# Forward substitution in VectorE's lanes on 16x16 blocks, two to a lane, instead of 32x32, with the block under the diagonal made by small TensorE products

## The chip, the cores and the metric

One core of one Trainium2 chip runs the whole program. The metric is the device time of one execution in microseconds. The kernel before takes 839.43 us in the median of three runs (832.2 to 842.1).

## The reference

An attention layer with a recurrent state is followed by an MLP. For each of 4 x 8 (batch, head) pairs the state is a 40 x 40 matrix; 768 steps of time update it:

```python
y[:, :, t] = np.einsum('bhd,bhde->bhe', rt, state)
Sa = np.einsum('bhde,bhe->bhd', state, at)
state_decay = state * wt[:, :, None, :] - np.einsum('bhd,bhe->bhde', Sa, bt)
state = state_decay + np.einsum('bhd,bhe->bhde', vt, kt)
```

The MLP takes the 3072 rows of 320 values: `h = x @ w_in`, `g = h * tanh(softplus(h))`, `out = g @ w_out`, with a width of 2048 between. All data is f32.

## The kernel before

**Chunks.** Time is cut into 12 chunks of 64 steps. Within a chunk the recurrence is written as matrix products, which needs the inverse of a triangular 64x64 matrix for each pair of batch and head. That matrix is handled as two diagonal 32x32 blocks, which are inverted, and a block under them, which is made by products.

**Three kinds of work.** `pre_a(c, be)` (line 126) prepares chunk c for half of the pairs: it loads w, a, b and k, forms the running products of the decay by scans on VectorE (lines 147 and 157), scales a (152) and b, k (170), stores the decays (172, through the POOL queue), and makes on TensorE (186) the products of a with b and k, from which the triangular matrices go to `gp` (lines 188, 189, 193), other parts to `ha` (190, 191). `inv(n)` (line 381) inverts the matrices of chunks 2n and 2n+1 at once; it is `pre_inv(n)` followed by `post_inv(n)`. `step(c)` (line 349) carries the state through chunk c: L284 multiplies the matrices KT with the state, L314, L334 and L339 make the chunk's output and the new state, L346 writes the state ST; step c+1 needs it.

**The inversion.** In `pre_inv` (line 205) a transpose by 32x32 blocks on VectorE (L209) brings the 128 matrices of 32x32 into lanes, one matrix to each of the 128 partitions: the tile X (named XL) is [128, 32, 32]. L210 writes ones on the diagonal. The loop of lines 211 to 216 is forward substitution: for i from 1 to 30 it multiplies column i under the diagonal with row i (L214, into `tmp`) and adds the (31-i) x i products (L216), each instruction waiting for the one before. L218 transposes back to TT, L220 also writes the plain transpose of half of it to T1, in place over a part of `gp`.

`post_inv` (line 223) makes, for each of the two chunks (h), 32 products of 32x32 (L232), a copy of them by ScalarE (L235), 32 more (L241), puts the blocks together in `bdT` (L249, L250 from TT, L251 from the products), multiplies with `ha` (L258) and copies the result to KT (L260), which `step` reads at L284.

**Buffers.** X, TT and `tmp` have one buffer each (`NXL`, `NTT`, `NTMP` are 1), `gp` two. The PSUM pool `ps_a` has two banks (`NA = 2`), which all products of `post_inv` share.

**Order.** The program is written down as step 2n, `pre_a` for the chunks of pair n + 2, `inv(n + 1)`, step 2n + 1 (`ORDER`, line 36). A scheduler then orders each engine's instructions by priority and by its estimate of what is ready; each engine carries them out in that fixed order. `at(tc, k)` gives the instructions under it the offset `OFF[k]` (line 38) in that priority: 80 for every inversion (`'I'`), and one of its own for each (`I0` 600, `I1` -15, and so on). Once the last `pre_a` is done, its memory is freed and the MLP's weights are loaded and split into two parts (lines 453 to 495); the MLP then follows, 12 pieces of 256 rows.

Of the kernel before, what the change touches and what calls it, by code (L numbers as in the profile page):

```python
# [7 lines left out]
F32 = mybir.dt.float32  # L8
F32R = mybir.dt.float32r
AF = mybir.ActivationFunctionType  # L10
ALU = mybir.AluOpType
# [20 lines left out]
NTMP = 1  # L32
# [4 lines left out]

OFF = {'I': 80, 'T1': 80, 'P00': -40, 'P10': 80, 'P11': 40, 'b0': 15, 'c0': 600, 'u0': -15, 'u1': 250, 'd0': 250,
       'd1': 150, 'W': 600, 'V': 400, 'E': 150, 'I0': 600, 'I1': -15, 'I2': 15, 'I3': 150, 'I4': 80, 'p4': 15,
# [4 lines left out]
def at(tc, k):  # L44
    return tc.high_priority(offset=OFF[k]) if OFF.get(k) else nullcontext()
# [33 lines left out]
def attention(ctx, tc, I, yD, pD, nch, M):  # L79
    nc = tc.nc  # L80
    V, A, PE, SP, G = nc.vector, nc.scalar, nc.tensor, nc.sync, nc.gpsimd
# [4 lines left out]
    ps_a = pool("ps_a", NA, ictx, "right", space=PSUM)  # L86
# [4 lines left out]
    ci = pool("ci", 1, ictx)  # L91
    iw = pool("iw", 2, ictx)
# [9 lines left out]
    bkb = [cp.tile([128, 8, 168], F32, name=f"bk{i}") for i in range(NWA)]  # L102
    adb = [cp.tile([128, 8, 2, 2, 32], F32, name=f"ad{i}") for i in range(NAD)] * (2 // NAD)
    d1 = cp.tile([128, 584], F32, name="d1")
    bdT = [ci.tile([128, 8, 2, 64], F32, name=f"bdT{i}") for i in range(2)]
    z = cs.tile([128, 1], F32, name="z")
    V.memset(z, 0.0)
# [97 lines left out]
    def pre_inv(n):  # L205
        gp = GP[n]

        X = iw.tile([128, 32, 32], F32, name="XL", bufs=NXL)
        V.transpose(X.rearrange("p t j -> p j t"), gp[:, :, 1].rearrange("p u j -> p j u"))  # L209
        V.memset(X.rearrange("p t j -> p (t j)")[:, 0:1024:33], 1.0)  # L210
        for i in range(1, 31):
            tmp = iw.tile([128, 240], F32, name="tmp", bufs=NTMP)
            tv = tmp[:, 0:(31 - i) * i].rearrange("p (t j) -> p t j", j=i)
            V.tensor_tensor(out=tv, in0=X[:, i + 1:32, i:i + 1].broadcast_to([128, 31 - i, i]),  # L214
                            in1=X[:, i:i + 1, 0:i].broadcast_to([128, 31 - i, i]), op=ALU.mult)
            V.tensor_tensor(out=X[:, i + 1:32, 0:i], in0=X[:, i + 1:32, 0:i], in1=tv, op=ALU.add)  # L216
        TT = iw.tile([128, 32, 32], F32, name="TT", bufs=NTT)
        V.transpose(TT.rearrange("p u t -> p t u"), X)  # L218
        T1 = gp[0:64, :, 0]
        V.transpose(T1, TT[0:64])  # L220
        return TT, T1

    def post_inv(n, TT, T1):
        gp = GP[n]
        for h in range(2):
            with at(tc, 'T%d' % h):
# [10 lines left out]
                for j in range(16):  # L237
                    u = h * 16 + j
                    for al in range(2):
                        q = slice(al * 32, 32 + al * 32)  # L240
                        PE.matmul(py[q, j], T1[q, u], X[q, j], start=(j == 0), stop=True, skip_group_check=True)  # L241
                for be in range(2):
# [138 lines left out]
    def inv(n):  # L381
        with at(tc, 'I%d' % n), at(tc, 'I'):
            TT, T1 = pre_inv(n)
        with at(tc, 'J%d' % n):
            post_inv(n, TT, T1)
# [93 lines left out]
class Mlp:  # L479
# [6 lines left out]
    def pool(self, n, b, side="right", **k):  # L486
        return self.ctx.enter_context(self.tc.tile_pool(name=n, bufs=b, side=side, **k))
# [140 lines left out]
def build(tc, I, out, nch):  # L628
    with ExitStack() as ctx:
        dp = ctx.enter_context(tc.tile_pool(name="dp", bufs=1, space=bass.MemoryType.DRAM))  # L630
        yD = dp.tile([nch, 2, 40, 2, 512], F32, name="yD")
        pD = dp.tile([nch, 2, 40, 2, 520], F32, name="pD")
        M = Mlp(ctx, tc, I, yD, pD, out)
        with ExitStack() as actx:
            attention(actx, tc, I, yD, pD, nch, M)
        M.run(nch)
# [21 lines left out]
```

## Time and profile before

| | |
|---|---|
| median of three runs | 839.43 us (832.2 to 842.1) |
| span of the profiled execution, first to last instruction | 843.5 us |
| mean granted TensorE clock over it | 0.939 |
| VectorE in L214 and L216, all six inversions | 58.5 and 59.0 us, 180 instructions each |
| TensorE in L232 and L241 | 768 records each |
| ScalarE busy | 429.0 us (51%) |

The profiled execution's time is its span; a separate clock of that one execution is not at hand, so it stands beside the runs, 4.1 us above their median.

In a profile, PE is TensorE's matmul, PEld its weight loads, DVE VectorE, ACT ScalarE, POOL GpSimd, SP SyncE. A group's line gives line, engine, operation, out<-in, partitions x elements, count, busy us, mean ns of one, and the idle time ahead of it with what ended it. A timeline's line gives start and duration in us, and in brackets the idle time before. A stretch's line gives its bounds and length, then for each engine the busy us and the number of instructions, then the granted TensorE clock, the share of the DMA engines and GB/s. In the rows of slices each digit is the busy share, in tenths, of a fortieth of the span (21 us).

### The profile page before, as it was taken

The page shows a single profiled execution, that of the slowest core. Times are in us where ns is not written, and L with a number is a line of the kernel's source. Part 1 is how long each engine was busy: PE and PEld are TensorE (multiplying, and loading weights), DVE is VectorE, ACT ScalarE, POOL GpSimd, SP SyncE. Part 2 cuts the span into 40 slices and gives each one's busy share as a digit, 9 for nine tenths or more (in the row PEclk, how much of TensorE's full clock was granted, in tenths as well). Part 3 has the DMA queues.
Part 4 walks back from the last instruction along what each step waited for, and adds up shares of the span by engine and source line. Part 5 has one row for each costly group of instructions (what it writes and reads, how often), then busy time and mean ns, then how long its engine had stood idle before and what let it go on. Part 6 is the DMA issues. An engine that isn't in the chain of part 4 may idle for free.

```text
span 843.5 us, 18796 instructions
## 1 busy us (share of the span) xinstructions
PE 748.6 (89%) x7816; PEld 695.6 (82%) x7816; DVE 462.0 (55%) x975; ACT 429.0 (51%) x937; POOL 103.3 (12%) x182
## 2 busy tenths in 40 slices
PE   2645898998989889889799899999999999999998
PEld 2534697887868778778768799999999999999998
DVE  6789879739899658788924639221222222122110
ACT  4533647774586866566738546333333333333331
POOL 8100012113122023221101200000000000000000
PEclk9855689899999999899959999999999999999999
DMA  6422223323423233323425734211120111100000
GB/s 177 134 71 64 74 63 73 90 67 105 129 81 80 66 88 103 82 67 96 123 66 142 179 109 128 54 35 36 38 54 25 31 54 35 35 21 16 16 1 32
DMA packets 58212, 61.91 MB, mean 73 GB/s; under 512 B 25536, under 2 KB 48704, under 8 KB 58128
## 3 DMA queue, kind: packets, MB, share of 16 engines
q1 hardware_dynamic: 49296, 40.94, 17.6%
q0 software_dynamic: 8832, 19.79, 9.5%
q8 instruction: 61, 1.00, 0.5%
q14 instruction: 23, 0.19, 0.1%
HBM read 48.79 MB, written 11.86 MB: 72 GB/s over the span
## 4 chain that ended last, share of the span: by engine, by line
PE 62%; DVE 15%; ACT 15%; issue 5%; DMA 2%; ACTq 0%; DVEq 0%; SPq 0%
PE ph L583 21%; PE po L604 7%; PE po L605 7%; PE po L603 7%; PE pa L186 5%; PE pa L258 4%; PE pq L314 3%; PE pq L334 2%; DVE XL L216 2%; DVE tmp L214 2%; ACT ad L155 2%; PE pu L284 1%; DMA cv_d<-in_wo 1%; DVE P L147 1%; ACT bdT L250 1%
## 5 line engine op out<-in xcount | busy, mean ns | idle before, releaser
L583 PE MATMUL ph<-xh,w_ih 128*128 128x256 f32 x576 | 148.3, 283 | 0.5 <-ACT xh L566 0.5
L585 ACT ACTIVATE g<-ph 128x512 f32<-128x512 f32 x96 | 57.3, 598 | 179.3 <-PE ph L583 179.2
L589 DVE TENSOR_TENSOR gl<-g,gh 128x1024 fp32r<-128x1024 f32 x48 | 58.7, 1225 | 160.7 <-ACT gh L588 160.4
L583 PE MATMUL ph<-xh,w_il 128*128 128x256 f32 x576 | 123.6, 283 | 0.0
L186 PE MATMUL pa<-bk,ad 128*128 128x168 f32 x384 | 85.0, 373 | 42.7 <-DVE bk L170 15.0
L604 PE MATMUL po<-w_ol,gh 128*128 128x320 f32 x384 | 118.8, 310 | 0.1
L605 PE MATMUL po<-w_oh,gl 128*128 128x320 f32 x384 | 118.4, 309 | 0.0
L603 PE MATMUL po<-w_oh,gh 128*128 128x320 f32 x384 | 117.7, 309 | 0.0
L186 PEld LDWEIGHTS pa<-bk,ad 128*128 128x128 f32 x384 | 70.8, 233 | 47.8 <-issue 22.8
L583 PEld LDWEIGHTS ph<-xh,w_ih 128*128 128x128 f32 x576 | 109.3, 190 | 0.7 <-ACT xh L566 0.7
L583 PE MATMUL ph<-xl,w_ih 128*128 128x256 f32 x384 | 101.2, 285 | 0.0
L583 PEld LDWEIGHTS ph<-xh,w_il 128*128 128x128 f32 x576 | 96.3, 190 | 0.0
L583 PEld LDWEIGHTS ph<-xl,w_ih 128*128 128x128 f32 x384 | 73.1, 190 | 0.8 <-issue 0.5
L604 PEld LDWEIGHTS po<-w_ol,gh 128*128 128x128 f32 x384 | 72.1, 188 | 0.5 <-DVE w_ol L495 0.5
L605 PEld LDWEIGHTS po<-w_oh,gl 128*128 128x128 f32 x384 | 72.1, 188 | 0.1
L603 PEld LDWEIGHTS po<-w_oh,gh 128*128 128x128 f32 x384 | 71.8, 188 | 0.0
L258 PE MATMUL pa<-bdT,HA 128*104 128x128 f32 x384 | 57.0, 304 | 9.0 <-ACT bdT L251 7.3
L258 PEld LDWEIGHTS pa<-bdT,HA 128*104 128x104 f32 x384 | 49.9, 190 | 14.4 <-ACT bdT L251 9.1
L216 DVE TENSOR_TENSOR XL<-XL,tmp 128x30 f32<-128x30 f32 (+9 forms) x180 | 59.0, 328 | 2.4
L214 DVE TENSOR_TENSOR tmp<-XL 128x30 f32<-128x30 f32 (+9 forms) x180 | 58.5, 325 | 2.5
L314 PE MATMUL pq<-bdr,UVT 128*128 128x128 f32 x384 | 57.3, 294 | 2.3 <-DVE UVQ L316 1.5
L314 PEld LDWEIGHTS pq<-bdr,UVT 128*128 128x128 f32 x384 | 50.8, 205 | 4.0 <-DVE UVQ L316 1.9
(89 smaller groups left out, 1243.5 us busy)
## 6 DMA issues: line engine op xcount, KB each, us to landing
wa<-in_wa SPq DMA_DIRECT2D x48, 162.5 KB
bk<-in_bk SPq DMA_DIRECT2D x48, 160.0 KB
cv_d<-in_wi SPq DMA_DIRECT2D x12, 512.0 KB
cv_d<-in_wo SPq DMA_DIRECT2D x8, 640.0 KB
pD<-P POOLq DMA_DIRECT2D x48, 81.2 KB, 2.2
VS<-in_vN POOLq DMA_DIRECT2D x24, 160.0 KB, 3.6
UVT<-in_vD POOLq DMA_DIRECT2D x24, 160.0 KB, 3.9
bdr<-in_rD POOLq DMA_DIRECT2D x24, 160.0 KB, 4.4
```

Source lines behind the costliest of these rows:

```text
L155: A.copy(ad[q, :, :, al], a[q].rearrange("p (s k t) -> p s k t", k=2, t=32))
L186: PE.matmul(pt[:, j], ad[:, s0 + j].rearrange("p k a t -> p (k a t)"), bk[:, s0 + j], start=(j == 0), stop=True, skip_group_check=True)
L214: V.tensor_tensor(out=tv, in0=X[:, i + 1:32, i:i + 1].broadcast_to([128, 31 - i, i]), in1=X[:, i:i + 1, 0:i].broadcast_to([128, 31 - i, i] ...
L216: V.tensor_tensor(out=X[:, i + 1:32, 0:i], in0=X[:, i + 1:32, 0:i], in1=tv, op=ALU.add)
L258: PE.matmul(pk[:, j], ha[:, s0 + j], bd[:, s0 + j].rearrange("p a t -> p (a t)"), start=(j == 0), stop=True, skip_group_check=True)
L314: PE.matmul(pq[:, s], UVT[:, g * 4 + s, be * 128:be * 128 + 128], br[:, be, g * 4 + s].rearrange("p a t -> p (a t)"), start=(s == 0), stop ...
L583: PE.matmul(o, w, x, start=(j == 0 and n == 0), stop=(n == 7), skip_group_check=True)
L585: A.activation(g[:, f0:f0 + 2], ph, AF.Mish)
L589: V.tensor_tensor(out=gl, in0=g, in1=gh.bitcast(F32), op=ALU.subtract)
L603: PE.matmul(po[k], gh[:, j, t], oh, start=(f == 0), stop=False, skip_group_check=True)
L604: PE.matmul(po[k], gh[:, j, t], ol, start=False, stop=False, skip_group_check=True)
L605: PE.matmul(po[k], gl[:, j, t], oh, start=False, stop=(f == 15), skip_group_check=True)
```

## The change

The forward substitution runs on the two 16x16 blocks of the diagonal of each matrix at once: the access pattern's first free dimension is [528, 2], which steps from one block to the other (16 rows of 32 and 16 columns further), and the loop goes from 1 to 14. The lower left block of X is cleared first. L218 then gives a TT that has the two small inverses. The inverses' left columns are also transposed into a new tile TD (whose other columns stay zero). Two batches of 128 TensorE products of 32x32 with 16 columns, one product for each matrix, with a ScalarE copy between them, make the block under the diagonal in PSUM: the first multiplies the matrix in `gp` with columns 16 to 31 of TT, the second TD with the result. VectorE adds the second batch to TT. Both batches take their PSUM banks from `ps_a`; the copy X1 goes to the first half of X. T1 and `post_inv` follow as before.

```diff
@@ attention
+    TD = ci.tile([128, 32, 32], F32, name="TD")
+    G.memset(TD, 0.0)
@@ pre_inv
         V.memset(X.rearrange("p t j -> p (t j)")[:, 0:1024:33], 1.0)
-        for i in range(1, 31):
-            tmp = iw.tile([128, 240], F32, name="tmp", bufs=NTMP)
-            tv = tmp[:, 0:(31 - i) * i].rearrange("p (t j) -> p t j", j=i)
-            V.tensor_tensor(out=tv, in0=X[:, i + 1:32, i:i + 1].broadcast_to([128, 31 - i, i]),
-                            in1=X[:, i:i + 1, 0:i].broadcast_to([128, 31 - i, i]), op=ALU.mult)
-            V.tensor_tensor(out=X[:, i + 1:32, 0:i], in0=X[:, i + 1:32, 0:i], in1=tv, op=ALU.add)
+        V.memset(X[:, 16:32, 0:16], 0.0)
+
+        for i in range(1, 15):
+            m = 15 - i
+            tmp = iw.tile([128, 112], F32, name="tmp", bufs=NTMP)
+            tv = tmp[:, 0:2 * m * i].rearrange("p (b t j) -> p b t j", b=2, j=i)
+            x = X[:, 0:1, 0:1]
+            ap = lambda t, j, st, sj: bass.AP(x.tensor, x.offset + 32 * t + j, [x.ap[0], [528, 2], [st, m], [sj, i]])
+            V.tensor_tensor(out=tv, in0=ap(i + 1, i, 32, 0), in1=ap(i, 0, 0, 1), op=ALU.mult)
+            V.tensor_tensor(out=ap(i + 1, 0, 32, 1), in0=ap(i + 1, 0, 32, 1), in1=tv, op=ALU.add)
         TT = iw.tile([128, 32, 32], F32, name="TT", bufs=NTT)
         V.transpose(TT.rearrange("p u t -> p t u"), X)
+        V.transpose(TD[:, :, 0:16].rearrange("p u j -> p j u"), X[:, :, 0:16].rearrange("p t j -> p j t"))
+        px = ps_a.tile([128, 32, 16], F32, name="pa")
+        for u in range(32):
+            for q in (slice(g * 32, g * 32 + 32) for g in range(4)):
+                PE.matmul(px[q, u], gp[q, u, 1], TT[q, u, 16:32], start=(u == 0), stop=True, skip_group_check=True)
+        X1 = X.rearrange("p t j -> p (t j)")[:, 0:512].rearrange("p (u t) -> p u t", t=16)
+        A.copy(X1, px)
+        py = ps_a.tile([128, 32, 16], F32, name="pa")
+        for u in range(32):
+            for q in (slice(g * 32, g * 32 + 32) for g in range(4)):
+                PE.matmul(py[q, u], TD[q, u], X1[q, u], start=(u == 0), stop=True, skip_group_check=True)
+        V.tensor_tensor(out=TT[:, :, 16:32], in0=TT[:, :, 16:32], in1=py, op=ALU.add)
         T1 = gp[0:64, :, 0]
         V.transpose(T1, TT[0:64])
         return TT, T1
```

## The prediction

> **What bounds the kernel now.** I read the page first (busy time, slices), then a table of stretches cut at the six inversions, then the groups of VectorE's instructions by shape, then the timeline around the places where a recurrence step starts. From the page:
>
> ```profile
> span 843.5 us, 18796 instructions
> ...
> PE 748.6 (89%) x7816; PEld 695.6 (82%) x7816; DVE 462.0 (55%) x975; ACT 429.0 (51%) x937; POOL 103.3 (12%) x182
> ...
> PE   2645898998989889889799899999999999999998
> ...
> DVE  6789879739899658788924639221222222122110
> ...
> POOL 8100012113122023221101200000000000000000
> ```
>
> The 55% of VectorE is a mean over two halves: from slice 24 on (the MLP) TensorE is full and VectorE has a fifth of its time in use; ahead of it (attention) VectorE is at 7 to 9 tenths, and TensorE too. So the change, which touches attention only, must be priced there. The stretches below begin with a transpose into `XL` and end with the transpose at L220 (the two bounds of an inversion), but for the last, the MLP:
>
> ```profile
> core 0: us, PE busy (x) PEld busy (x) DVE busy (x) ACT busy (x) POOL busy (x), PEclk, DMA share, GB/s
> 49.90:100.50 50.60, 27.32 (x164) 22.68 (x164) 47.00 (x118) 20.30 (x59) 5.07 (x10) 0.62 0.23 69
> 100.50:153.50 53.00, 48.48 (x640) 43.22 (x634) 45.44 (x113) 35.01 (x90) 9.95 (x18) 0.88 0.31 75
> 186.80:237.20 50.40, 43.55 (x565) 38.48 (x563) 47.64 (x127) 29.26 (x81) 15.23 (x27) 1.00 0.41 109
> 237.20:280.60 43.40, 37.33 (x594) 32.45 (x594) 40.03 (x104) 32.01 (x80) 8.56 (x16) 1.00 0.27 75
> 321.30:370.80 49.50, 44.83 (x503) 39.89 (x504) 43.86 (x117) 27.09 (x75) 12.91 (x23) 0.93 0.33 80
> 370.80:419.60 48.80, 41.37 (x727) 36.72 (x726) 41.80 (x107) 36.10 (x84) 7.82 (x12) 0.97 0.40 112
> 485.00:843.50 358.50, 354.75 (x2758) 353.51 (x2757) 95.59 (x102) 130.42 (x190) 1.00 (x2) 1.00 0.15 42
> ```
>
> VectorE is busy for 47.0 of 50.6 us in the first inversion, 47.6 of 50.4 in the third, 86 to 92% in the others. But TensorE is at 85 to 91% in all except the first (54%); its busy time is modelled, so I read this as "close to full", not full. Two engines bind in turn.
>
> Does the end of an inversion start anything? These rows are from the timeline: the state of the step before (ST), the KT that comes from the inversion, and the first matmul of the next step (L284).
>
> ```profile
> 235.60 0.48 DVE L346 TENSOR_TENSOR ST<-stn,R 128x320 f32<-128x320 f32 x1
> 246.00 0.55 PEld L284 LDWEIGHTS pu<-KT,VS 104*64 104x64 f32 x16 [0.18 <-ACT KT L260]
> ...
> 314.06 0.49 DVE L346 TENSOR_TENSOR ST<-stn,R 128x320 f32<-128x320 f32 x1
> 315.78 0.28 PE L284 MATMUL pu<-KT,VS 104*64 104x64 f32 x2
> ...
> 370.77 0.44 DVE L346 TENSOR_TENSOR ST<-stn,R 128x320 f32<-128x320 f32 x1
> 380.06 0.58 ACT L260 COPY KT<-pa 104x512 f32<-104x512 f32 x1 [0.74 <-PE pa L258]
> 381.66 1.12 PE L284 MATMUL pu<-KT,VS 104*64 104x64 f32 x16
> ```
>
> Step 4 starts 9.9 us after its state was there, released by KT: the inversion sets it. Step 8 likewise starts 10.5 us after its state, just behind KT. Step 6 starts 1.2 us after the state: there the recurrence sets the time and not the inversion.
>
> **VectorE, per inversion.** Groups by line and shape:
>
> ```profile
> L216 DVE TENSOR_TENSOR XL<-XL,tmp 128x30 f32<-128x30 f32 (+9 forms) x180 | 59.0, 328 | 2.4
> L214 DVE TENSOR_TENSOR tmp<-XL 128x30 f32<-128x30 f32 (+9 forms) x180 | 58.5, 325 | 2.5
> ...
> L214 DVE TENSOR_TENSOR tmp<-XL 128x30 f32<-128x30 f32 x12 | 2.1, 176 | 0.2
> L216 DVE TENSOR_TENSOR XL<-XL,tmp 128x108 f32<-128x108 f32 x12 | 3.2, 268 | 0.2
> ...
> L209 DVE STREAM_TRANSPOSE XL<-GP 128x1024 f32<-128x1024 f32 x6 | 12.7, 2124 | 0.0
> L218 DVE STREAM_TRANSPOSE TT<-XL 128x1024 f32<-128x1024 f32 x6 | 11.8, 1970 | 0.1
> L316 DVE TENSOR_TENSOR UVQ<-pq,cst 128x512 f32<-128x512 f32 x48 | 32.9, 688 | 24.4 <-PE pq L314 24.3
> L109 DVE MEMSET wa<- 128x1040 f32 x2 | 1.9, 925 | 0.4 <-issue 0.4
> ```
>
> Removed: 60 instructions, (59.0 + 58.5) / 6 = 19.6 us. Added in their place: 28 of 2(15-i)i elements, 28 to 112 (1120 in all for each of the two lines). From 176 ns at 30 and 268 at 108 elements an instruction costs 141 ns and 1.18 ns per element: 28 x 0.141 + 2240 x 0.00118 = 6.6 us. The clear of 16 x 16 is a quarter of L109's elements, 0.25 us. TD is the transpose of half a tile: half of 1.97 to 2.12, 1.0 us. The closing add reads 512 elements from PSUM as L316 does: 0.69 us. Net -19.6 + 6.6 + 0.25 + 1.0 + 0.69 = -11.1 us for each of 6 inversions, 66 us of VectorE. That price is sure to about 1 us. The one clear of TD goes to POOL at the start, where the slices show 8 tenths for 21 us and next to nothing after; TD is first read after 53 us, so I cost it at nothing (a few us if its place in the queue held up a load).
>
> **TensorE, per inversion.** 256 products of 32x32 weights with 16 columns. Lines 232 and 241 make 32 such products with 32 columns per half, and the trace has 64 records for them: an f32 product is two records. So 512 records are added. Rows of the timeline, the first inversion and the last, and the group of the ScalarE copy between two such batches:
>
> ```profile
> 99.24 1.82 PE L232 MATMUL pa<-TT,GP 32*32 32x32 f32 x64 [0.24 <-DVE TT L218]
> ...
> 418.23 1.20 PE L232 MATMUL pa<-TT,GP 32*32 32x32 f32 x64 [0.30 <-DVE TT L218]
> ...
> L235 ACT COPY X<-pa 64x512 f32<-64x512 f32 x12 | 6.9, 575 | 0.2
> ```
>
> 64 records take 1.20 us at full clock, 1.82 in the first inversion, where the table shows a clock of 0.62. At these prices 512 cost 9.6 us (14.6 in the first): 62 us in all. The new batches go round four tiles instead of two and stream half the columns, which no row here shows; the lower bound is half the price, 4.8 us, the upper one is under rival 2. I take 9.6, the nearest row.
>
> **Latency.** Nothing after an inversion may use TT before the add. Behind the transpose to TT now come 4.8 us (first batch), 0.58 (copy to X1, on ScalarE as L235), 4.8 (second batch), 0.69 (add): 10.9 us at full clock, 15.9 in the first inversion. TD's transpose lies beside the first batch. The loop in front is 13.0 us shorter (19.6 - 6.6). So a lone inversion would end 2 us earlier, 3 later in the first. What can be gained beyond that comes from other VectorE work that is laid into those 11 to 16 us: the first stretch has 47.0 us busy, of which the inversion's own transposes and loop make
>
> ```profile
> sum 285.30, DVE 141.92; mean DVE 23.65
> ```
>
> 23.65 us (the view of the stretches for tile XL alone), so 23 us of other work to lay there. The add is a new wait on VectorE: it stands there until the last product, and in order behind it wait whatever the scheduler put next, the masks of line 191 (which free TensorE's other banks) and those of L316 (which the steps need) first of all; the 0.69 us are charged, such a blockage is part of rival 3. The new batches take the two `ps_a` banks in turn, and X is free only after the second batch; the next inversion's L209 stands behind that, but it starts later than this anyway in every case before (187 against 153, 321 against 281), except for the second, fourth and sixth, which follow within 5 us.
>
> **The sum, stretch by stretch.** First: VectorE-bound, TensorE half idle: -11.1, of which 3 are lost as uncovered latency: -8; nothing runs ahead of step 0, so all of it comes through. Second: 11.1 off an engine with 7.6 us idle, 9.6 on one with 4.5 idle: 0. Third: step 4 can move by at most 9.9, and TensorE pays 9.6: -5, half of it. Fourth: step 6 waits for the state, so VectorE's relief is worth nothing; a third of TensorE's 9.6 falls between matmuls of steps 4 and 5: +3. Fifth: as the third, with more TensorE time: -4. Sixth: a third of 9.6 again: +3. Products that the scheduler lays one by one between other matmuls (rival 2): 15 in all at 0.34, +5. Sum -8 + 0 - 5 + 3 - 4 + 3 + 5 = -6 us. The MLP's 358.5 us stay. The profiled execution's span of 843.5 becomes 837.5; it stands 4.1 above the median of 839.4 (its runs go from 832.2 to 842.1), so on the median's scale I forecast 833.4 us.
>
> **Rival 1: the small products cost little.** If four tiles run at once, a batch takes half (4.8 us per inversion): the latency falls to 6 us, and the stretches become -9, -4, -8, 0, -6, 0, with no charge for interleaving: -27, 812 us. For it: the 16 columns, the four row groups. Against: the rows of 64 in 1.20 us already have two tiles. [...] Chance 0.22.
>
> **Rival 2, slower: products laid one by one between other matmuls.** Where the scheduler alternates them, the timeline shows
>
> ```profile
> 395.54 0.94 PE L334 MATMUL pq<-UVQ,bkn 128*64 128x104 f32 x16
> ...
> 422.14 0.39 PE L334 MATMUL pq<-UVQ,bkn 128*64 128x104 f32 x2
> 422.46 0.24 PE L241 MATMUL pa<-X,GP 32*32 32x32 f32 x2
> 422.64 0.39 PE L334 MATMUL pq<-UVQ,bkn 128*64 128x104 f32 x2
> 422.96 0.24 PE L241 MATMUL pa<-X,GP 32*32 32x32 f32 x2
> ```
>
> From 422.14 to 422.64 is one pair of each: 0.50 us, against 0.12 (0.94 / 8) and 0.04 (1.20 / 32) in a block: 0.34 us lost per alternation. With 256 new products per inversion instead of the 128 of L232 and L241, under a priority that lets them in among the steps, twelve alternations per inversion on the path cost 6 x 12 x 0.34 = 24.5 us in place of my 5: 833.4 - 5 + 24.5 = 853 us. It decides over the gain from about 33 alternations (11 us of gain before this charge). For it: the last inversion has a dozen such in a row. Against: most batches of L232 ran as blocks. [...] Chance 0.24.
>
> **Rival 3: the inverse comes no earlier.** If nothing is laid into the new latency, the terms of the first, third and fifth stretch (-17) vanish: +11, 844 to 850 with a part of it. The waits at L316 (24.4 us idle in its row) speak for it: VectorE stands in order behind TensorE. Chance 0.14. That the rewritten loop does not shorten VectorE's time can be left out: its prices come from the same instructions.
>
> **Chances and range.** Forecast 0.40, with its own range 824 to 843; rivals 0.22, 0.24, 0.14. 1% is 8.4 us, about what the three runs before could tell. Faster by more (under 831): all of rival 1 and 0.4 of the forecast, 0.38. Slower by more (over 848): most of rival 2 and half of rival 3, 0.30. Within: 0.32. The range goes from below rival 1 to above rival 2: 808 to 860.
>
> **What would show it.** VectorE's busy time falls from 462 to about 396; the group of the loop from 117 us to 40; TensorE has 3072 more records, at 19 ns in blocks. The first products on TT come before 90 us (99.24 now). Step 4 starts 3 to 8 us earlier relative to the inversion's start. If 256 records of a batch take under 3 us, rival 1 holds; if they are strewn over 8 us or more between L284, L314 or L334, rival 2. The forecast is wrong if the MLP's stretch changes, or if the time leaves 824 to 843.

## The result, and the profile after

The changed kernel takes 940.94 us in the median of four runs (934.27 to 944.62), the kernel before 840.76 us in four (832.2 to 842.23). The ratio is 1.118, with a 95% interval from 1.110 to 1.126: about 100 us slower, where 6 us faster had been forecast. Below, "+70 us" for a kernel means its ratio to the kernel before less 1, times 840.76.

The page of the kernel after has a span of 942.8 us:

```profile
span 942.8 us, 24795 instructions
...
PE 824.4 (87%) x10888; PEld 762.9 (81%) x10888; DVE 411.8 (44%) x801; ACT 434.5 (46%) x943; POOL 104.3 (11%) x183
...
DVE  6795288362366324583147455651222212222111
...
PEclk9775998778796958996898699999999999999999
...
q8 instruction: 85, 1.39, 0.6%
```

The two rows of the page before that the prediction did not use:

```profile
PEclk9855689899999999899959999999999999999999
...
q8 instruction: 61, 1.00, 0.5%
```

VectorE now has many slices of 2 to 5 tenths in attention, and yet attention is longer. TensorE has 3072 records more (10888 against 7816), its clock stands at 5 to 8 tenths in many slices of attention where most had 8 or 9, and 24 more packets went over the instruction queue (85 against 61): 6144 TensorE instructions more (a weight load and a matmul for each record), so by my estimate 256 to a packet (6144 / 24).

Where the time went is read from stretches that run from the start of one inversion to that of the next (the sixth to the start of the MLP). Before:

```profile
49.90:101.80 51.90, 28.50 (x179) 23.39 (x177) 48.30 (x119) 21.52 (x62) 5.07 (x10) 0.62 0.23 67
101.80:186.80 85.00, 78.01 (x1113) 69.98 (x1113) 58.95 (x145) 58.30 (x148) 16.00 (x29) 0.89 0.31 76
186.80:241.90 55.10, 46.98 (x641) 41.12 (x639) 51.18 (x133) 33.72 (x94) 15.23 (x27) 1.00 0.40 108
241.90:321.30 79.40, 69.36 (x1087) 61.60 (x1084) 57.92 (x142) 57.87 (x147) 15.92 (x29) 1.00 0.30 78
321.30:375.20 53.90, 48.36 (x578) 42.76 (x578) 45.66 (x122) 31.29 (x89) 12.91 (x23) 0.94 0.33 78
375.20:485.00 109.80, 98.21 (x1362) 82.34 (x1361) 69.97 (x153) 70.46 (x148) 17.67 (x26) 0.89 0.47 122
```

After:

```profile
49.00:126.70 77.70, 56.81 (x1152) 50.21 (x1150) 44.15 (x103) 39.84 (x105) 10.73 (x20) 0.78 0.24 64
126.70:184.90 58.20, 50.46 (x819) 40.87 (x818) 40.27 (x99) 25.86 (x73) 10.00 (x18) 0.82 0.32 87
184.90:284.50 99.60, 86.78 (x1385) 74.44 (x1383) 49.47 (x114) 48.40 (x123) 16.60 (x30) 0.83 0.24 67
284.50:395.20 110.70, 91.15 (x1711) 80.52 (x1711) 49.07 (x108) 60.60 (x152) 14.86 (x27) 0.78 0.20 51
395.20:485.00 89.80, 83.60 (x1435) 72.69 (x1434) 37.20 (x94) 48.85 (x127) 15.30 (x27) 0.83 0.22 54
485.00:585.00 100.00, 78.53 (x1531) 71.58 (x1531) 60.88 (x123) 54.26 (x111) 15.28 (x22) 0.85 0.45 122
585.00:942.80 357.80, 354.07 (x2753) 353.03 (x2753) 96.12 (x104) 131.12 (x191) 1.00 (x2) 1.00 0.16 44
```

All of the loss lies in attention: 435.1 us from the first inversion to the MLP before, 536.0 after, while the MLP's 358 us stand. The pieces of work do not fall into the same stretch in both kernels, so pairs must be taken together: the first two stretches are 136.9 and 135.9 us, the next two 134.5 and 210.3, the last two 163.7 and 189.8. VectorE's busy time is lower in every pair (107.3 to 84.4, 109.1 to 98.5, 115.6 to 98.1 us); the clock, 0.89 to 1.00 from the second stretch on, is 0.78 to 0.85.

The timeline of TensorE behind the first inversion:

```profile
69.40 1.79 PE L229 MATMUL pa<-TT,GP 32*32 32x16 f32 x193 [0.38 <-DVE TT L224]
73.63 0.71 PE L229 MATMUL pa<-TT,GP 32*32 32x16 f32 x63 [2.44 <-issue]
74.27 1.49 PE L188 MATMUL pa<-bk,ad 128*128 128x168 f32 x6
75.69 1.03 PE L235 MATMUL pa<-XL,TD 32*32 32x16 f32 x59
77.63 1.90 PE L235 MATMUL pa<-XL,TD 32*32 32x16 f32 x128 [0.91 <-issue]
81.36 1.15 PE L235 MATMUL pa<-XL,TD 32*32 32x16 f32 x69 [1.83 <-issue]
...
84.15 1.92 PE L250 MATMUL pa<-TT,GP 32*32 32x32 f32 x64
```

The records themselves are quick, 193 in 1.79 us (9.3 ns each). But TensorE stands still three times, for 0.9 to 2.4 us, waiting for nothing that the profile shows ("issue"). From the first stop to the second it does 63 + 59 = 122 of these records and, between the batches, 6 of L188: 128 in all. From the second to the third it does 128. 128 records are 256 instructions, by that estimate one packet of the instruction queue. Here the first product on the finished TT (L250) comes at 84.15 us, 15 us before the 99.24 of the kernel before.

The third inversion looks different. First its L229 alone, in the table of stretches, then rows of the timeline:

```profile
215.00:272.50 57.50, 10.53 (x256) 7.01 (x256) 0.82 0.26 71
```

```profile
215.66 0.23 PE L229 MATMUL pa<-TT,GP 32*32 32x16 f32 x2
215.82 0.49 PE L332 MATMUL pq<-bdr,UVT 128*128 128x128 f32 x2
216.24 0.23 PE L229 MATMUL pa<-TT,GP 32*32 32x16 f32 x2
...
301.72 1.02 PE L302 MATMUL pu<-KT,VS 104*64 104x64 f32 x14
```

One batch of 256 records is spread over 57.5 us, part of it in pairs of records between pairs of the step's matmuls (0.58 us from pair to pair). Step 4, which is waiting for this inverse, starts at 301.72, 116.8 us after the inversion's start at 184.9; before, it was 246.0 less 186.8 = 59.2 us.

### The profile page after: what moved, and what is told of

The parts are those of the page before. It is cut to its first block, busy times and chain, and to the rows that moved or that the text cites. A ratio compares the mean times of both kernels' runs of the same rounds, so it can differ in the third digit from the quotient of the medians.

```text
span 942.8 us, 24795 instructions
## 1 busy us (share of the span) xinstructions
PE 824.4 (87%) x10888; PEld 762.9 (81%) x10888; DVE 411.8 (44%) x801; ACT 434.5 (46%) x943; POOL 104.3 (11%) x183
## 4 chain that ended last, share of the span: by engine, by line
PE 70%; DVE 11%; ACT 9%; issue 6%; DMA 3%; SPq 0%; ACTq 0%; DVEq 0%
PE ph L601 19%; PE pa L188 6%; PE po L622 6%; PE po L623 6%; PE po L621 6%; PE pa L276 4%; PE pq L332 3%; PE pu L302 3%; PE pa L235 3%; PE pq L352 2%; PE pa L229 2%; DMA cv_d<-in_wi 2%; PE pa L204 2%; PE pu L311 2%; DVE P L149 2%
## 5 line engine op out<-in xcount | busy, mean ns | idle before, releaser
L188 PE MATMUL pa<-bk,ad 128*128 128x168 f32 x384 | 91.8, 388 | 38.2 <-DVE bk L172 16.0
L188 PEld LDWEIGHTS pa<-bk,ad 128*128 128x128 f32 x384 | 72.9, 239 | 42.9 <-issue 23.1
L276 PE MATMUL pa<-bdT,HA 128*104 128x128 f32 x384 | 61.2, 322 | 7.2 <-ACT bdT L269 4.9
L334 DVE TENSOR_TENSOR UVQ<-pq,cst 128x512 f32<-128x512 f32 x48 | 32.7, 687 | 75.3 <-PE pq L332 75.3
L276 PEld LDWEIGHTS pa<-bdT,HA 128*104 128x104 f32 x384 | 55.9, 208 | 9.6 <-ACT bdT L269 6.3
L352 PE MATMUL pq<-UVQ,bkn 128*64 128x104 f32 (+1 forms) x768 | 48.6, 259 | 6.2 <-ACT yev L361 4.5
## 6 DMA issues: line engine op xcount, KB each, us to landing
cv_d<-in_wi SPq DMA_DIRECT2D x12, 512.0 KB
```

What stands on the lines that cost most here:

```text
L188: PE.matmul(pt[:, j], ad[:, s0 + j].rearrange("p k a t -> p (k a t)"), bk[:, s0 + j], start=(j == 0), stop=True, skip_group_check=True)
L276: PE.matmul(pk[:, j], ha[:, s0 + j], bd[:, s0 + j].rearrange("p a t -> p (a t)"), start=(j == 0), stop=True, skip_group_check=True)
L334: V.tensor_tensor(out=UVQ[be][:, g * 8:g * 8 + 8, 0:64], in0=pq.rearrange("p s (a t) -> p (s a) t", a=2), in1=maskQ.unsqueeze(1).broadcast ...
L352: PE.matmul(py[be * 64:be * 64 + 64, 2 * j + al, 0:n], BKN[c, be][:, u * 40:u * 40 + 64], UVQ[be][:, u, 0:n], start=(j == 0 and al == 0), ...
```

## The experiments

Each kernel below keeps the MLP and the steps as they are.

**hi600: all products in uninterrupted blocks.** The lines from the first batch to T1 get the offset 600 in priority:

```diff
-        px = ps_a.tile([128, 32, 16], F32, name="pa")
-        ...
-        V.transpose(T1, TT[0:64])
+        with tc.high_priority(offset=600):
+            px = ps_a.tile([128, 32, 16], F32, name="pa")
+            ...
+            V.transpose(T1, TT[0:64])
```

> The changed kernel, with both batches of products, the copy between them, the add and the T1 transpose moved up 600 places in the scheduler's priority, so that each batch of 128 products stands as one block in TensorE's order. Theory A (order: the products lie strewn among the steps' matmuls, the inverse comes late, and each alternation costs some 0.4 us): most of the 100 us goes, 835 to 870 us. Rival B (the products cost TensorE too much wherever they stand: records and waits for instructions, some 55 us): 890 to 940 us.

912.14 us (909.87 to 918.88), ratio 1.083 [1.077, 1.090]: +70 us. As rival B asked (890 to 940), and theory A (835 to 870) falls: strewing the products costs some 29 us of the 99, and the rest remains where nothing is strewn. On TensorE the new products lie in 12 pieces here, each without another record between, and in 99 in the changed kernel. Stretches of TensorE drawn around the twelve blocks (first the two of inversions 1 and 3, then the sum over all twelve, with about 0.1 us of margin on each side):

```profile
68.70:73.80 5.10, 2.63 (x257) 0.97 0.31 86
75.50:81.40 5.90, 4.08 (x258) 0.50 0.32 90
...
201.30:204.10 2.80, 2.69 (x257) 0.85 0.02 6
207.20:213.30 6.10, 4.24 (x258) 0.50 0.01 3
...
sum 68.10, PE 43.79; mean PE 3.65
```

So twelve blocks take 68.1 less 2.4 us of margins, 65.7 us: 21.4 ns for each of 3072 records. The busy time of 43.8 us takes in some records of the margins. By the groups, 23.9 + 18.0 = 41.9 us are the products' own records (14 ns each), and the other 23.8 us are waits that the profile does not explain (12.3 + 11.5, "issue"):

```profile
L236 PE MATMUL pa<-XL,TD 32*32 32x16 f32 x1536 | 23.9, 210 | 12.6 <-issue 12.3 <-ACT XL L232 0.3
L230 PE MATMUL pa<-TT,GP 32*32 32x16 f32 x1536 | 18.0, 192 | 15.0 <-issue 11.5 <-DVE TT L224 3.5
```

The second block of each of the six inversions runs at clock 0.50.

**dve_only: the shorter loop alone.** TD, both batches, the copy and the add are left out, so the block under the diagonal stays zero and TT lacks it.

```diff
-        V.transpose(TD[:, :, 0:16].rearrange("p u j -> p j u"), X[:, :, 0:16].rearrange("p t j -> p j t"))
-        px = ps_a.tile([128, 32, 16], F32, name="pa")
-        ...
-        V.tensor_tensor(out=TT[:, :, 16:32], in0=TT[:, :, 16:32], in1=py, op=ALU.add)
```

> The changed kernel without the TD transpose, the products, the copy and the add: the block under the diagonal of each 32x32 inverse stays zero. Both theories: the shorter loop by itself gives time back, 800 to 830 us, since the inversions set the start of half of the steps. A third theory, C (VectorE's time is worth nothing because the schedule is bound elsewhere, and a shorter loop only lets the scheduler set the preparation of later chunks behind other work): 835 us or more.

828.97 us (826.45 to 832.4), ratio 0.983 [0.978, 0.988]: 14 us less (10 to 18), inside the 800 to 830 that both theories asked. VectorE's busy time falls by 66 us to 395.9, and only a fifth of that shows in the time. The group of the masks shows where some of it went:

```profile
L191 DVE TENSOR_TENSOR HA<-pa,cst 128x192 f32<-128x192 f32 (+1 forms) x72 | 23.7, 329 | 60.3 <-ACT HA L190 59.1 <-PE pa L186 1.0
```

Ahead of L191 VectorE was idle for 25.7 us in the kernel before and is for 60.3 here: relieved of the loop it waits for ScalarE.

**pe_off: the products alone, needed by nobody.** The kernel before (loop of 32) makes both batches as well, with `gp` as weights of the second, and copies their result into the half of X that is free; everything is computed as before, beside that.

```diff
         V.transpose(TT.rearrange("p u t -> p t u"), X)
+        ...
+        A.copy(X1, px)
+        ...
+        V.tensor_copy(X.rearrange("p t j -> p (t j)")[:, 512:1024].rearrange("p (u t) -> p u t", t=16), py)
```

> The kernel before, its loop over 32 untouched, with two batches of 128 such products added per inversion whose results go nowhere (they are copied into X, which is no longer read), so nothing waits for them but the next inversion. Theory A: the priority lets them fall into gaps, but strewn as they are they still cost alternations: 860 to 890 us. Rival B: the full TensorE price, 890 us or more. If under 850 us, neither the products nor their order cost much off the chain, and the lateness of the inverse is all.

938.75 us (938.38 to 939.12), ratio 1.113 [1.107, 1.119]: +95 us, nearly all of the change's loss, with the long loop. As rival B asked (890 or more). But the products are not off the chain in this kernel, though nothing reads their copy. X has one buffer, and VectorE, in its fixed order, stands still for 43.3 us in five waits at the copy of their results (L229). The second batch of inversion 2 ends at 229.7 us, and then come:

```profile
229.70 0.69 DVE L229 COPY XL<-pa 128x512 f32<-128x512 f32 x1 [0.61 <-PE pa L228]
...
230.86 2.13 DVE L209 STREAM_TRANSPOSE XL<-GP 128x1024 f32<-128x1024 f32 x1
...
258.50 0.48 DVE L357 TENSOR_TENSOR ST<-stn,R 128x320 f32<-128x320 f32 x1
...
293.30 0.59 ACT L271 COPY KT<-pa 104x512 f32<-104x512 f32 x1 [3.10 <-PE pa L269]
...
294.26 1.12 PE L295 MATMUL pu<-KT,VS 104*64 104x64 f32 x16
```

Inversion 3 (L209) starts only behind that copy, at 230.9 (186.8 before), and step 4 starts on KT, 35 us after its state was there; steps 8 and 10 likewise 25 us after theirs. So pe_off shows that the products cost as much beside the long loop. It does not tell their time on TensorE from the lateness of the inverse.

**pe_chain: the products on the chain, with the long loop.** As pe_off, but the second batch times zero is added to TT, so that everything after waits for it.

```diff
-        V.tensor_copy(X.rearrange("p t j -> p (t j)")[:, 512:1024].rearrange("p (u t) -> p u t", t=16), py)
+        V.scalar_tensor_tensor(out=TT[:, :, 16:32], in0=py, scalar=0.0, in1=TT[:, :, 16:32], op0=ALU.mult, op1=ALU.add)
```

> As the run with products whose results go nowhere, but the second batch times zero is added to TT, so that the rest of the inversion waits for it as in the changed kernel; the loop over 32 stays. Theory A: the wait is the main cost, so 950 us or more (100 us of change, and VectorE's 66 us not saved). Rival B: about what the run without the wait gives, plus at most 6 times 11 us of latency.

917.84 us (912.58 to 923.11), ratio 1.088 [1.079, 1.097]: +74 us, less than with the products off the chain. My theory that a wait on the chain is what costs had asked for 950 us and more, and falls. The scheduler put these products in 71 pieces on TensorE and those that nobody needs in 193, so the two kernels differ in more than the wait.

**half and one: fewer products.** As hi600, with every second u left out (half) or all but u = 0 (one, 8 products per inversion, of 256). The parts of the block under the diagonal that are not made stay zero. Theory D in the expectations, that what costs is the halved clock after the small products, is set out at full128.

```diff
-            for u in range(32):
+            for u in range(0, 32, 2):
```

> The run with 600 places with every second product of each batch left out (64 in place of 128; every second block under the diagonal stays zero). Between 829 us (no products) and 912 us (all): theory B, which goes by instructions, says the middle, 865 to 880 us. [...]

> The run with 600 places with one product for each group of 32 partitions per batch, 8 in all per inversion in place of 256; copy and add shrink to these (nearly all blocks under the diagonal stay zero). What is left is the chain of handovers between TensorE, ScalarE and VectorE and the TD transpose. Theory E (the longer chain to TT is what costs): 870 us or more. Theories B and D: 830 to 842 us.

half: 875.36 us (875.18 to 875.53), ratio 1.038 [1.031, 1.045], +32 us, half-way as theory B had it. one: 842.74 us (840.18 to 849.6), ratio 1.007 [1.002, 1.012], +6 us, where theory E asked 870 or more; it falls.

Between dve_only and one lie 20 us for the handovers (TD, copy, add, and the waits between engines) with next to no products. one also has the offset of 600, and no run separates what that does by itself. So even if all 256 products were free, the change with its products in blocks would gain nothing. From one to half to hi600 the cost grows by 26 and 38 us: in all 63.8 us for 2976 records, 21.4 ns each. From the first record of each block to its last, the twelve blocks come to 3.2 us in one, 24.8 in half and 65.7 in hi600, that is 62.5 us more in hi600 than in one. In sum, then, the time grows by the length of the blocks, and nothing of them is hidden.

**wide64: the clock brought back.** As hi600, but each product streams 64 columns in place of 16, and the result is added times zero, so that the block under the diagonal stays zero.

```diff
-PE.matmul(px[q, u], gp[q, u, 1], TT[q, u, 16:32], start=(u == 0), stop=True, skip_group_check=True)
+PE.matmul(px[q, u % 8 * 4:u % 8 * 4 + 4].rearrange("p a b -> p (a b)"), gp[q, u, 1], TT[q, u // 2 * 2:u // 2 * 2 + 2].rearrange("p a b -> p (a b)"), start=(u == 0), stop=True, skip_group_check=True)
```

> The run with 600 places, as many products and records, but each streams 64 columns in place of 16 (the results overlap and are added times zero). [...] Theory D: the clock stays higher, 0.93 or more over the span, and the time falls under 900 us although TensorE works more. Theory B with the wait for instructions as its core: the waits vanish behind the longer products, a batch takes some 7.5 us in place of 5.5, and the time is 915 to 935 us.

904.43 us (903.59 to 905.27), ratio 1.073 [1.065, 1.080], +61 us. The blocks of inversion 1 and the sum of the twelve:

```profile
69.90:75.40 5.50, 4.13 (x257) 1.00 0.34 89
...
76.20:82.90 6.70, 4.38 (x258) 1.00 0.28 81
...
sum 73.40, PE 53.19; mean PE 4.43
```

The clock stays at 1.00 in nine of the twelve blocks (0.62, 0.91 and 0.94 in the others), and over the span it is 0.947, where hi600 has 0.904 and the kernel before 0.939. The blocks are 5.3 us longer than in hi600 and the whole 9 us shorter, with intervals that overlap; the 900 us below which the clock would have been a main cause are missed by 4. If the longer blocks cost their 5.3 us in full, the lower clock is worth, by my estimate, some 14 us (9 + 5.3) of hi600's 70, and the bulk stands without it. Theory B's range (915 to 935) is missed too: the waits do not vanish behind the longer products, 19.5 us of "issue" remain in the two lines. Here the time does not follow the blocks in full: they are 68 us longer than those of one, and the whole is 55 us longer.

**full128: one full-height product in place of four.** As hi600, with 32 products per batch whose weights are the 128x128 identity; the result is added times zero.

```diff
-                for q in (slice(g * 32, g * 32 + 32) for g in range(4)):
-                    PE.matmul(px[q, u], gp[q, u, 1], TT[q, u, 16:32], start=(u == 0), stop=True, skip_group_check=True)
+                PE.matmul(px[:, u], ident, TT[:, u, 16:32], start=(u == 0), stop=True, skip_group_check=True)
```

> The changed kernel with the products moved up 600 places, but each batch is 32 products with the 128x128 identity as weights and 16 columns in place of 128 with 32x32 weights, and the result is added times zero (the block under the diagonal stays zero). A quarter of the instructions, and every product fills the array. Theory D (the small products leave the array so empty that its clock is halved after them; 153 us of half clock in the run with 600 places against 61 us without products): the clock recovers to 0.93 or more and the time falls to 835 to 860 us. Theory B (TensorE's own time for records and waits for instructions): a batch of 64 records at the price of a 128-column weight load, some 7 us, costs what it cost before, 890 to 915 us.

995.84 us (992.64 to 999.03), ratio 1.181 [1.169, 1.193], +152 us. Both theories asked for 915 us at most and missed. A quarter of the records, but each far longer:

```profile
69.30 12.06 PE L229 MATMUL pa<-TT,cst 128*128 128x16 f32 x64 [0.39 <-DVE TT L224]
...
82.46 13.67 PE L234 MATMUL pa<-XL,cst 128*128 128x16 f32 x64
```

188 and 214 ns per record of 16 columns, at a granted clock of 0.58 and 0.50 in these two stretches. The twelve blocks come to 146.1 us, over twice the 65.7 of the small records they stand for. The time is 146 us above that of one: again the length of the blocks, with a quarter of the records.

**bf16hi and bf16: one record per product.** The operands are the upper halves of the f32 words, read as bf16, so that a product is one record; the block under the diagonal has 8-bit mantissas. bf16hi has the offset of hi600, bf16 the priority of the changed kernel. The scheduler did not keep bf16hi's products in uninterrupted blocks: they lie in 29 pieces on TensorE (hi600's in 12), those of bf16 in 91 (the changed kernel's in 99).

```diff
-PE.matmul(px[q, u], gp[q, u, 1], TT[q, u, 16:32], start=(u == 0), stop=True, skip_group_check=True)
+PE.matmul(px[q, u], gp[q, u, 1].bitcast(BF16)[:, 1::2], TT[q, u, 16:32].bitcast(BF16)[:, 1::2], start=(u == 0), stop=True, skip_group_check=True)
```

> All 128 products per batch, in uninterrupted blocks as with offset 600, but with the upper halves of the f32 words as bf16 operands: one record (a weight load and a matmul) per product instead of two, 1536 added records in place of 3072; the block under the diagonal is computed with 8-bit mantissas. Theory R (the price goes with TensorE's records and their instructions, about 20 ns of the path each): as with half of the products, ratio 1.03 to 1.05, 865 to 882 us; 12 extra instruction fetches instead of 24. Rival P (the price goes with the products, their tile changes and their streams of 16 columns, whatever the number of passes): as with offset 600, ratio 1.07 to 1.09, 898 to 916 us. Rival F (f32 passes themselves are what is slow, a bf16 pass much shorter): near the kernel with 8 products, ratio 1.005 to 1.02, 842 to 856 us.

> The same bf16 products in the priority of the changed kernel, where they may be strewn between the step's matmuls. If the cost of the order (29 us between the changed kernel and offset 600) goes with the number of alternations of kinds, it stays: 890 to 912 us, 20 to 35 us above the blocks of bf16. If it goes with the number of records, it halves: 10 to 15 us above the blocks, 877 to 895 us.

bf16hi: 884.25 us (877.71 to 890.57), ratio 1.052 [1.042, 1.063], +44 us. bf16: 893.31 us (889.35 to 897.17), ratio 1.065 [1.054, 1.076], +54 us. The full number of products with half of the records lies nearest to half (+32), 2 us above the range of theory R, and well under the 898 us of theory P. The groups of bf16hi:

```profile
L237 PE MATMUL pa<-XL,TD 32*32 32x16 bf16 x768 | 10.7, 173 | 10.2 <-issue 7.0 <-ACT XL L233 3.2
...
L231 PE MATMUL pa<-TT,GP 32*32 32x16 bf16 x768 | 7.0, 171 | 4.1 <-DVE TT L225 4.1
```

TensorE's busy time in the two lines falls from 41.9 us to 17.7 and its unexplained waits from 23.8 us to 7.0. bf16hi's pieces come to 24.8 us, like half's blocks, but it takes 12 us more than half, with intervals that overlap; why stays open.

The order of the changed kernel costs 10 us over bf16hi, where it cost 29 with f32. That is near the 10 to 15 that were asked if this part goes with the records, and under the 20 to 35 if it goes with the alternations. But the runs of the two kernels overlap, and bf16hi is strewn a little itself, so this is a hint and no proof.

## Why the prediction was wrong

**VectorE: right.** The groups of the kernel after:

```profile
L221 DVE TENSOR_TENSOR tmp<-XL 128x28 f32<-128x28 f32 (+6 forms) x84 | 19.6, 233 | 1.3
L222 DVE TENSOR_TENSOR XL<-XL,tmp 128x28 f32<-128x28 f32 (+6 forms) x84 | 19.6, 233 | 1.2
...
L225 DVE STREAM_TRANSPOSE TD<-XL 128x512 f32<-128x512 f32 x6 | 6.6, 1093 | 0.1
...
L236 DVE TENSOR_TENSOR TT<-TT,pa 128x512 f32<-128x512 f32 x6 | 4.1, 685 | 12.0 <-PE pa L235 12.0
```

The loop is 39.2 us against the 40 forecast, TD 1.09 us against 1.0, the add 0.685 against 0.69. In the page the busy time falls by 50 us, to 411.8, and not by 66 to the 396 forecast, since the records of successive short instructions overlap and the page counts overlap once: the durations themselves sum to 512.0 us before and 446.4 after, 66 less. What this is worth in the time, 14 us by dve_only, is near the 17 that the first, third and fifth stretch were to gain. That is luck: the 17 already had the new latency and TensorE's price taken off, and dve_only has neither.

**TensorE's price: the size right, its composition wrong.** 9.6 us per inversion were charged at 19 ns a record, for hi600 65.7 / 6 = 10.9 us were measured, and 21.4 ns. But it is not 19 ns of work: in the rows above the records take 9 to 18 ns, and the rest are stops, which I had not considered and which lie 128 records apart in the rows behind the first inversion. Rival 1 looked at the records alone: the fastest run in these rows, 193 records in 1.79 us, gives 9.3 ns, half of the 19 charged. A batch in a block takes 5.5 us in the mean of hi600's twelve; one of them (201.3 us) stays under the 3 that rival 1 needed. It is refuted.

**The failed step: "The sum, stretch by stretch".** It took TensorE's 9.6 us per inversion to be covered in the first stretch by the idle half of TensorE, and counted "a third of TensorE's 9.6" in the fourth and sixth, since the rest was to fall between matmuls. Measured on the path is the whole: 63.8 us for the 2976 records that hi600 has over one. I had read idle TensorE time of 9 to 46% as room. It was not room.

That this cost does not come from the inverse's own chain shows in hi600: steps 6, 8 and 10 start on their state, which comes 17 to 18 us after the last of their KT. Step 10:

```profile
493.63 1.07 ACT L279 COPY KT<-pa 104x512 f32<-104x512 f32 x2
...
512.48 0.48 DVE L365 TENSOR_TENSOR ST<-stn,R 128x320 f32<-128x320 f32 x1
...
513.88 1.10 PE L303 MATMUL pu<-KT,VS 104*64 104x64 f32 x32
```

In one these three steps start on the state too. From the start of step 6 to that of step 10 it takes 131.2 us in one (312.1 to 443.3) and 160.0 in hi600 (353.9 to 513.9). The four blocks of inversions 5 and 6, which lie between, are 24 us longer in hi600, and 29 us appear in the time although no step there waits for their result. That the cost goes by the length of the blocks is shown by half, hi600 and full128 against one; wide64 comes out 13 us under it.

Why not even a part was hidden is my reading, and no run isolates it: a block of 5 us holds up the steps' and preparations' matmuls behind it in TensorE's fixed order, and the gaps in which TensorE waits for other engines come again after it. VectorE also stands still at the add until a block ends (25.0 us in hi600, 4.5 in one), and no run tells its part from TensorE's.

The first stretch's gain, of which "all of it comes through", was there and was lost: in the changed kernel step 0 starts at 93.7 us, 16 earlier than before, but step 2 at 205.2, 31 later. It starts on KT, 27 us after its state; the products of its inversion end at 184.2.

**The handovers.** "Behind the transpose to TT" 10.9 us were added and 13.0 taken away in front. In the first inversion the chain from the first product to the end of the add takes 69.40 to 83.25 us, 13.9 us, against the 15.9 forecast for it. Yet the chain with next to no products (one against dve_only) costs 20 us in all, 3.4 us per inversion; in the forecast the same parts (copy 0.58, add 0.69, TD 1.0) came to 2.3 us, and were partly covered. By itself this eats VectorE's 14 us: with next to no products the outcome lies in the range of rival 3, 844 to 850 us (one: 846 on that scale), though rival 3 comes to it by other terms.

**The order.** "15 in all at 0.34, +5" was charged; hi600 against the change measures 29 us, near the 24.5 of rival 2. Its sign was there (a batch strewn over 57.5 us, where 8 were named), and its price fits: 87 pieces more than in hi600, at 0.34 us, are 30 us. Its mechanism is not shown by that. In the changed kernel steps 2, 4 and 10 also start on KT, 22 to 27 us after their state, so the late inverse may be the cost as well. In two other pairs the price comes out at twice the difference: 122 pieces between pe_off and pe_chain are 41 us by it and 21 measured, 62 between bf16 and bf16hi 21 and 10. And rival 2 stood on a sum that was already 81 us too low without this part (-11 against +70): its 853 us would have been wrong too.

The balance of the 99 us, each term from a difference of two runs with some 6 us of uncertainty: the shorter loop -14, the handovers +20, the products in blocks +64 (of which the lower clock, by the estimate from wide64, some 14), their strewn order +29. Of "what would show it", the loop, the 3072 records and the 90 us were met; VectorE's 396 us were missed on the page; the price of a block came out as forecast, though not for the reason given; step 4 came 58 us later relative to its inversion, not 3 to 8 us earlier.

## What to carry to other kernels

A busy share of 85% on an in-order engine that many chains share was not 15% of room here: price new work on it in full, and take something off only where the trace shows a gap with nothing behind it in the order. Price many tiny matmuls per instruction and not per column: 3072 more records here cost 21 ns each in blocks and 31 ns as the scheduler laid them ((99.4 - 6.2) / 2976), although a record ran in 9 to 18, and with four times the columns the blocks grew by 8% only. Before moving work from an engine, try what its removal alone is worth: the 66 us that dve_only takes from VectorE's busy time were worth 14, less than the 20 between it and one.

## What the runs showed of the hardware

**Dense small matmuls stopped 128 records apart behind the first inversion.** The instruction queue had 24 packets more for 3072 records more (12 for the 1536 of half, 6 for the 768 of full128), which is 128 records or 256 instructions to a packet, and the stops of 0.9 to 2.4 us behind the first inversion lie 128 records apart where records run at 9 to 18 ns. In hi600 23.8 us of TensorE's waits in these lines remain visible, in bf16hi 7.0. That these waits are for the fetch of instructions is not shown: I infer it from their spacing, since the profile names no releaser.

**The clock fell in the batches of small matmuls.** In all of hi600's second batches of 16 columns the granted clock is 0.50, though TensorE is busy for 4.0 us or more in each; with 64 columns it stays at 1.00 in nine of twelve batches. With 128x128 weights and 16 columns it is low too: 0.50 in all six second batches of full128, whose mean is the lowest of all, 0.862. The small gain of wide64 says that it mattered less here than its row of slices suggests.

**With 128x128 weights a record of 16 columns took far longer.** With 128x128 f32 weights 16 columns take 188 to 214 ns per record in the two batches shown, at clock 0.58 and 0.50. The twelve batches take 146.1 us for 768 records, 190 ns each, nine times the 21.4 of a 32x32 one in hi600's blocks; the shortest, at clock 0.83, takes 8.5 us, 133 ns each.
